# Attention and gated FFN on one core: a new written order, waits between two engines, and tanh queued behind copies

## The chip, the cores and the metric

The kernel runs on one core of a Trainium2 chip. The metric is the device time of one execution in microseconds (us). A core has TensorE (PE: matmuls; PEld: its weight loads), VectorE (DVE), ScalarE (ACT), GpSimd (POOL) and SyncE (SP, which issues most DMAs). Each engine runs its instructions in the order of its own queue; semaphores hold an instruction until another engine's has finished.

## The reference

Block-local attention with block summaries, then a feed-forward layer with a convolution gate, on 4 batches, 8 heads, 768 positions, head size 64 (model width 512, inner width 1024).

```python
def _attn_ref(q, k, v):                      # B, H, S, D = 4, 8, 768, 64
    block, window = (32, 16)
    k_sum = k.reshape(B, H, nb, block, D).max(axis=3)
    v_sum = v.reshape(B, H, nb, block, D).mean(axis=3)
    scores_l = scale * q @ k.T               # kept where |i - j| < window
    scores_s = scale * q @ k_sum.T + np.log(block)
    a = softmax(concat(scores_l, scores_s))
    return a @ concat(v, v_sum)

def _moe_ref(x, w_in, conv_w, w_out):        # x: heads side by side, 512 wide
    h = np.maximum(x @ w_in, 0.0)
    conv_out = sum(conv_w[k] * shifted(h, k - 1) for k in range(3))
    gate = 1.0 / (1.0 + np.exp(-conv_out))
    return (h * gate) @ w_out
```

## The kernel before

The work is cut into 8 chunks (4 batches, two halves of 384 positions each). Attention goes by pairs of heads: pair n belongs to chunk n // 4. The FFN of chunk c runs in 8 units u of 128 inner features. FFN products are split into high and low fp32r parts, so each step of f (first product, `L467`) and of the second product (`L554`) is three matmuls.

The steps have short names, and a written list, ORDER, uses them. Attention: R, K, T, V, Q, M load (SP queue); `ks` takes key maxima over blocks (`L291`, DVE), `vs` value sums (`L307`, DVE), `pv` transposes the sums (`L317`, PE, into the one PSUM bank x), `vm` scales them out of PSUM (`L335`), `kb`, `vb` and `win` copy summaries and key windows into tiles (`L301`, `L341`, `L297`); `qk` is scores (`L354`, PE), `mx` maximum with mask (`L368`, DVE), `ex` exp (`L383`, ACT), `sm`, `rc`, `nr` the normalisation, `tr` the transpose (`L411`, PE), `cp` its copy aT (`L416`), `av` values (`L425`, PE, into bank x), `xh`, `xl` the two parts of x (`L451`, `L455`). Group j of tr and cp is half of pair j // 2. FFN: `f`, `re` relu, `ta` and two `cv` the taps (`L504`), `th` tanh (`L515`, ACT), `mu` the product (`L522`, DVE), `gh` and `gl` its two parts (`L532`, `L535`), `g` a step of the second product, `ob` its way out. Unit (c, u) takes one of three f1 PSUM banks, which is free again after its mu. Weights are unpacked by `z`, `lo` (`L176`), `st` (`L182`), `hi`, `wl` (`L202`). `w` is a number of filler matmuls. A letter at the end of a step (a, v, p) names the engine: ScalarE, VectorE, GpSimd.

Chunks 0 to 2 of the FFN and the attention of pairs 0 to 17 stand in ORDER, and every engine takes that order. From chunk 3 (FIRST) on, a loop emits the units, and there only TensorE's order is as written (`manual_schedule(engines={PE})`); the other queues are ordered by a scheduler that goes by costs. The loop's slot j (j = 8 (c + 1) + 3 + u) loads and prepares: an odd slot vs, pv, vm, ks and kb of pair (j + 1) / 2, an even one the scores and softmax of pair j / 2. In chunk 3 each slot's instructions are put behind the last DMA and the last mu of ORDER on their engine:

```python
with contextlib.ExitStack() as behind:
    if c == FIRST:
        for x in last.values():
            behind.enter_context(tc.issue_after(x))
    slot(j)
```

The first odd slot is 35: pair 18. After it come tr33, the gates (th, mu, gh, gl) of the unit before, the four f steps of unit (3,0) and nine matmuls of the second product; unit (3,1) begins with tr34, av16, slot 36 (qk18) and tr35.

Of the kernel before, what the change touches and what calls it, by code (L numbers as in the profile page):

```python
# [9 lines left out]
F32 = mybir.dt.float32  # L10
# [8 lines left out]
P = 128  # L19
# [73 lines left out]
ex13.0.0 f1.7.3 mx13.1.2 cp23a cv1.6.2 f2.0.1 ex13.0.2 rc12 nr12.0p re1.7 av11 th1.6 gl1.5
ex13.1.1 tr24 mu1.6 ex13.1.2 g2.3 ta1.7v ex13.0.1 nr12.1p f2.0.2 xh11 cv1.7.0 qk14 xl11 cv1.7.2
f2.1.0 K17 cp24v th1.7 g2.4 M15 mx14.0.0 gh1.6 mu1.7 K16 sm13 pv17 gl1.6 f2.0.3 mx14.0.1 T18
mx14.0.2 tr25 re2.0 f2.2.0 ex14.0.1 ta2.0v f2.1.1 gh1.7 mx14.1.0 g2.5 cv2.0.0 ex14.0.0 gl1.7
cp25a mx14.1.1 f2.1.2 cv2.0.2 vm17 g2.6 rc13 th2.0 ks16 nr13.0p ex14.1.0 f2.1.3 ex14.1.1 nr13.1p
mx14.1.2 R18 tr26 mu2.0 f2.2.1 Q16 kb16 gh2.0 pv16 qk15 re2.1 ex14.0.2 g2.7 cp26a mx15.0.0 K18
mx15.0.1 f2.2.2 ta2.1v ob2 f2.3.0 cv2.1.0 f2.2.3 mx15.0.2 cv2.1.2 g3.0 re2.2 vm16 f2.3.1 th2.1
ex14.1.2 tr27 f2.3.2 sm14 mx15.1.0 mx15.1.1 g3.1 mx15.1.2 mu2.1 f2.3.3 ta2.2v gh2.1 g3.2 rc14  # L100
cv2.2.0 nr14.0p av12 cv2.2.2 gl2.0 g3.3 xh12 nr14.1p ex15.0.1 f2.4.0 xl12 ex15.1.1 g3.4 th2.2
cp27a qk16 mu2.2 gh2.2 f2.4.1 re2.3 K19 gl2.2 f2.5.0 ta2.3a f2.4.2 ex15.0.2 kb17 tr28 g3.5
mx16.0.0 mx16.0.1 f2.4.3 cp28v mx16.0.2 g3.6 cv2.3.0 tr29 cv2.3.2 g3.7 mx16.1.0 mx16.1.1 f2.5.1
mx16.1.2 ob3 av13 ex15.0.0 g4.0 ex16.1.0 M17 cp29v ex15.1.2 f2.5.2 V15 ed12 re2.4 Q17 g4.1 xh13
Q18 ex15.1.0 xl13 f2.5.3 M16 ta2.4a g4.2 V16 sm15 th2.3 rc15 V17 cv2.4.0 nr15.1p av14 ex16.0.0
mu2.3 ex16.1.2 nr15.0p cv2.4.2 ex16.1.1 g4.3 ex16.0.1 tr30 gh2.3 g4.4 xh14 gl2.3 re2.5 qk17
# [9 lines left out]
def attention_ffn(ctx, tc, qT, kT, vT, k_win, v_nat, v_win, w_in, cwT, w_out, mask8, ident_in, out):  # L116
# [73 lines left out]
    def lo(kind, fc):  # L190
        lower(f"{kind}{fc}", DM)

    def st(kind, fc):
        joined(f"{kind}{fc}")

    def hi(kind, fc, e="a"):
        copy[e](parts(kind, fc)[0], wu[f"{kind}{fc}"].bitcast(F32))

    def wlo(kind, fc, e="p"):
        h, l = parts(kind, fc)  # L200
        w = wu.pop(f"{kind}{fc}")
        engine[e].tensor_tensor(l, w.bitcast(F32), h.bitcast(F32), ALU.subtract)  # L202
# [7 lines left out]
    def stcw():  # L210
        joined("cw")
# [587 lines left out]
```

## Time and profile before

| | us |
|---|---|
| median of 3 runs | 397.97 |
| the runs | 399.1, 397.97, 394.14 |
| profiled execution, its own time | 394.99 |
| its span, first to last instruction | 393.2 |
| PE, DVE, ACT, POOL busy | 371.7, 255.1, 246.4, 148.4 |
| mean granted TensorE clock | 0.986 |

The span is what the trace covers; the execution's own time has 1.8 us around it. Busy time of an engine is the union of its instructions. Matmuls are pipelined, so a busy TensorE is not one at its peak. The idle time of an engine that sets nothing costs nothing.

### The profile page before, as it was taken

The page shows a single profiled execution, that of the slowest core. Times are in us where ns is not written, and L with a number is a line of the kernel's source. Part 1 is how long each engine was busy: PE and PEld are TensorE (multiplying, and loading weights), DVE is VectorE, ACT ScalarE, POOL GpSimd, SP SyncE. Part 2 cuts the span into 40 slices and gives each one's busy share as a digit, 9 for nine tenths or more (in the row PEclk, how much of TensorE's full clock was granted, in tenths as well). Part 3 has the DMA queues.
Part 4 walks back from the last instruction along what each step waited for, and adds up shares of the span by engine and source line. Part 5 has one row for each costly group of instructions (what it writes and reads, how often), then busy time and mean ns, then how long its engine had stood idle before and what let it go on. Part 6 is the DMA issues. An engine that isn't in the chain of part 4 may idle for free.

```text
span 393.2 us, 8828 instructions
## 1 busy us (share of the span) xinstructions
PE 371.7 (95%) x3167; PEld 316.6 (81%) x3167; DVE 255.1 (65%) x776; ACT 246.4 (63%) x786; POOL 148.4 (38%) x183
## 2 busy tenths in 40 slices
PE   8899889999999992999989999999999999999996
PEld 3677677988888872888978888888988898999884
DVE  5999999997876465667575565466665655566200
ACT  3998989976965576246667777666766743344211
POOL 2756766854442153123323243333333132232200
PEclk9999999999999997699999999999999999999999
DMA  8999947997643660754433323334310000000011
GB/s 302 385 307 320 294 133 249 310 263 248 208 132 110 161 208 28 251 151 161 123 96 114 115 53 98 108 103 124 103 38 28 29 2 27 28 28 27 28 53 53
DMA packets 26859, 55.03 MB, mean 140 GB/s; under 512 B 3072, under 2 KB 11456, under 8 KB 26816
## 3 DMA queue, kind: packets, MB, share of 16 engines
q1 hardware_dynamic: 23072, 47.91, 38.9%
q10 hardware_dynamic: 3744, 6.57, 4.6%
q8 instruction: 25, 0.41, 0.4%
q14 instruction: 18, 0.15, 0.1%
HBM read 46.11 MB, written 6.29 MB: 133 GB/s over the span
## 4 chain that ended last, share of the span: by engine, by line
PE 74%; DVE 11%; DMA 7%; ACT 3%; issue 2%; SPq 1%; POOL 0%; ACTq 0%; DVEq 0%; POOLq 0%
PE f L554 32%; PE f L467 29%; PE xp L425 5%; PE pt L411 5%; PE pq L354 4%; DVE t L504 3%; DMA raw_b<-w_in 2%; DMA raw_a<-w_in 2%; DMA kw<-k_win 1%; DVE a L368 1%; ACT a L383 1%; DVE t L522 1%; DMA mask<-mask 1%; DVE ks L291 1%; ACT t L515 1%
## 5 line engine op out<-in xcount | busy, mean ns | idle before, releaser
L535 POOL TENSOR_TENSOR glo<-t,ghi 128x383 fp32r<-128x383 f32 (+1 forms) x64 | 65.6, 1027 | 122.1 <-ACT ghi L532 114.5
L467 PE MATMUL f<-xh,win_hi 128*128 128x384 f32 (+1 forms) x256 | 92.2, 360 | 0.9 <-DVE t L522 0.5
L467 PE MATMUL f<-xh,win_lo 128*128 128x384 f32 (+1 forms) x256 | 87.1, 340 | 0.0
L467 PE MATMUL f<-xl,win_hi 128*128 128x384 f32 (+1 forms) x256 | 87.1, 340 | 0.0
L504 DVE SCALAR_TENSOR_TENSOR t<-f,cw,t 128x382 f32<-128x382 f32 (+3 forms) x128 | 78.7, 615 | 9.9 <-ACT t L493 7.3
L554 PE MATMUL f<-wout_hi,ghi 128*128 128x512 f32 x192 | 77.2, 402 | 0.0
L383 ACT ACTIVATE a<-a,nm 128x120 f32<-128x120 f32 x192 | 73.5, 386 | 4.2 <-DVE nm L368 3.2
L554 PE MATMUL f<-wout_lo,ghi 128*128 128x512 f32 x192 | 75.6, 394 | 0.0
L554 PE MATMUL f<-wout_hi,glo 128*128 128x512 f32 x192 | 75.3, 393 | 0.0
L403 POOL TENSOR_TENSOR a<-a,sm 128x360 f32<-128x360 f32 x56 | 44.5, 810 | 52.8 <-DVE sm L399 35.4
L515 ACT ACTIVATE t<-t 128x383 f32<-128x383 f32 (+1 forms) x64 | 33.6, 524 | 48.6 <-DVE t L504 47.4
L467 PEld LDWEIGHTS f<-xh,win_hi 128*128 128x128 f32 x256 | 48.8, 191 | 5.9 <-DVE t L522 1.5
L522 DVE SCALAR_TENSOR_TENSOR t<-t,f 128x383 f32<-128x383 f32 (+1 forms) x64 | 35.3, 552 | 26.0 <-ACT t L515 25.7
L368 DVE CUSTOM_DVE_ANT_0 a<-pq,mask 128x120 f32<-128x120 f32 x192 | 44.5, 275 | 10.2 <-PE pt L411 5.3
L467 PEld LDWEIGHTS f<-xl,win_hi 128*128 128x128 f32 x256 | 48.9, 191 | 1.9
L467 PEld LDWEIGHTS f<-xh,win_lo 128*128 128x128 f32 x256 | 48.7, 190 | 0.0
L554 PEld LDWEIGHTS f<-wout_hi,glo 128*128 128x128 f32 x192 | 36.2, 188 | 8.0
L495 DVE TENSOR_SCALAR t<-f,cw 128x385 f32<-128x385 f32 (+1 forms) x42 | 25.9, 617 | 25.1 <-ACT f L482 21.2
L482 ACT ACTIVATE f<-f 128x384 f32<-128x384 f32 (+1 forms) x64 | 30.3, 474 | 17.5 <-PE f L467 17.1
L554 PEld LDWEIGHTS f<-wout_hi,ghi 128*128 128x128 f32 x192 | 36.4, 189 | 5.6 <-ACT ob L564 0.3
L554 PEld LDWEIGHTS f<-wout_lo,ghi 128*128 128x128 f32 x192 | 36.3, 189 | 4.8 <-POOL wout_lo L202 0.2
L532 ACT CAST ghi<-t 128x383 fp32r<-128x383 f32 (+1 forms) x64 | 32.5, 508 | 10.3 <-DVE t L522 10.3
(53 smaller groups left out, 470.6 us busy)
## 6 DMA issues: line engine op xcount, KB each, us to landing
va<-v_win SPq DMA_DIRECT2D x32, 288.0 KB
kw<-k_win SPq DMA_DIRECT2D x24, 360.0 KB
kT<-kT SPq DMA_DIRECT2D x16, 400.0 KB
q<-qT SPq DMA_DIRECT2D x32, 192.0 KB
out_dram<-ob ACTq DMA_DIRECT2D x24, 256.0 KB
vt<-vT SPq DMA_DIRECT2D x12, 384.0 KB
wo<-w_out SPq DMA_DIRECT2D x8, 512.0 KB
raw_a<-w_in SPq DMA_DIRECT2D x6, 512.0 KB
```

The costliest lines, as they stand in the source:

```text
L368: nc.vector.tensor_tensor_reduce(aa[n, h][:, i, :], pq[n][h][:, i * NK : (i + 1) * NK], mask[:, {(0, 0): 0, (1, 2): 2}.get((hf, i), 1), :] ...
L383: nc.scalar.activation(a, a, AF.Exp, bias=nm[n][:, h, i : i + 1], scale=-1.0, accum_out=sm[n][:, h, i : i + 1],)
L403: engine[e].tensor_tensor(a, a, sm[n][:, h, :].unsqueeze(2).to_broadcast([P, 3, NK]), ALU.mult)
L467: nc.tensor.matmul(f1ps[c, u][:, :n], w[:, u, cc, :], x[:, cc, :n], start=(cc == 0 and m == 0), stop=(cc == NCC - 1 and m == 2),)
L482: nc.scalar.activation(h, h, AF.Relu)
L495: nc.vector.tensor_scalar(t, h, cw[:, u, 1:2], 1.0, ALU.mult, ALU.mult)
L504: nc.vector.scalar_tensor_tensor(t[:, i0:i1], f1ps[c, u][:, hf + k - 1 + i0 : hf + k - 1 + i1], cw[:, u, k : k + 1], t[:, i0:i1], ALU.mult ...
L515: nc.scalar.activation(t, t, AF.Tanh, scale=0.5)
L522: return nc.vector.scalar_tensor_tensor(t, t, 1.0, h, ALU.add, ALU.mult)
L532: copy[e](gate_rows("hi", c, u), conv[c, u])
L535: engine[e].tensor_tensor(gate_rows("lo", c, u), conv.pop((c, u)), gate_rows("hi", c, u).bitcast(F32), ALU.subtract,)
L554: nc.tensor.matmul(f2ps[b, st], g[:, fc, ss], w[:, fc, :], start=(fc == 0 and m == 0), stop=(fc == NFC - 1 and m == 2),)
```

## The change

ORDER is written anew: the same steps in another sequence, many with another engine letter, with 30 filler matmuls in place of 35 (12 stand ahead of the list in both). A step may now carry a wait: `a<b` makes step a wait for step b, though it uses nothing of b. There are 43, each between VectorE and GpSimd: 15 hold a VectorE step behind a GpSimd one, 28 the other way. The steps of slot 35 (Q19, vs18, ks18, V18, pv18, vm18, kb18) move into ORDER. In even units of the loop the gates are queued behind the unit's first copy aT on the copy's engine. The functions that make the steps return their instruction so that it can be named; what counts as `last` stays the DMAs and mu.

```diff
 ORDER = """
-R0 Q0 R1 I1 R3 R2 Q1 ks0 I2 win0 T0 kb0 qk0 Q2 win1 ks1 I0 kb1 mx0.0.0 zi1 T1 loi1 mx0.0.1
...
-tr0 vm0 ex1.1.2 qk2 nr0.1v I6 cp0a loi0 sm1 tr1 hii2 mx2.0.0 win6 rc1 mx2.0.1 cp1a pv1 V1
...
-ob4 f2.6.3 sm17 gh2.5 rc17 nr17.0v re2.6 nr17.1p ta2.6a cv2.6.0 gl2.5 f2.7.0 cv2.6.2 gl2.4 th2.6
-f2.7.1 mu2.6 f2.7.2 f2.7.3 re2.7 ta2.7a cv2.7.0 cv2.7.2 th2.7 gh2.6 mu2.7 gl2.6 gh2.7 gl2.7
+R0 Q0 R1 R2 R3 Q1 I2 ks0 I1 Q2 kb0v win0 T0 qk0 ks1 I0 ks2 win2 Q3 win1 mx0.0.0 T1 mx0.0.1
...
+ex0.1.2 ex0.1.1 C loi2<win3 sm0 mx1.0.0 zi2 kb3<loi2 rc0 mx1.0.1 nr0.0p ex1.0.0 mx1.0.2 T2
+mx1.1.0 ex1.0.2 nr0.1p mx1.1.1 w5 tr0 ex1.0.1 mx1.1.2 V1 kb4v qk2 ex1.1.1 sti2<nr0.1p ex1.1.2 Q4
+ex1.1.0 cp0v win5<sti2 mx2.0.0 sm1 w1 tr1 zi1 rc1 loi1<win5 pv0 mx2.0.1 ex2.0.0 nr1.0p<loi1 O0
...
+gl1.7v g2.6 ex14.0.0 Q17 cv2.0.2 ex14.0.2 f2.2.2 ex14.1.2 mx15.0.0 mx15.0.1 av12 cp26a sm14p
...
+gl2.0 mx15.1.1 cv2.2.2 g3.2 xh13 vs17 ex15.1.0 f2.3.2 g3.3 mu2.1 T19 kb16v f2.3.3 mx15.1.2 xl13
+ex15.1.2 tr28 re2.3v qk16 cp28a gh2.1 pv17 f2.4.0 ex15.0.1 mx16.0.0 mx16.0.1 th2.2 g3.4 ex15.1.1
+mu2.2 tr29 sm15p vs18 gh2.2 g3.5 vm17 cp29a M17 f2.5.0 ta2.3v R19 f2.4.1 mx16.0.2 rc15 ex16.0.2
...
+nr16.1p<gl2.3v ex17.1.1 g4.5 xl14 th2.4 gl2.1 ta2.5v tr32 g4.6 mu2.4 cp32a cv2.5.0 ex17.1.0 av15
+sm17 rc17 cv2.5.2 nr17.1p g4.7 th2.5 f2.6.2 xh15 mu2.5 xl15 f2.6.3 re2.6 ta2.6v cv2.6.0 nr17.0v
+f2.7.0 cv2.6.2 gh2.4p<nr17.0v ob4 gl2.4 th2.6 gh2.5v<gl2.4 mu2.6 gl2.5<gh2.5v f2.7.1 f2.7.2
+f2.7.3 re2.7v pv18 ta2.7v cv2.7.0 gh2.6v cv2.7.2 vm18v th2.7 gl2.6v mu2.7 gh2.7 gl2.7
 """
...
-    last = {}
+    last, made = {}, {}
+    held = mybir.DependencyInfo(
+        mybir.DependencyClass.Sync, mybir.DependencyReason.SCHED_ONLY
+    )
...
     def run(text):
+        text, *first = text.split("<")
...
         if x is not None:
-            last[x.ins.engine] = x.ins
+            made[text] = x.ins
+            if name in "KRTQVMOIC" or name == "mu":
+                last[x.ins.engine] = x.ins
+            for y in first:
+                tc.add_manual_dep(x.ins, made[y].name, held, reason="shared port")
...
     def slot_t(j):
         if 0 <= j - 2 < NGROUP:
             tr(j - 2)
-            cpy(j - 2)
+            return cpy(j - 2)
...
     def unit(c, u, pieces):
         j = 8 * (c + 1) + 3 + u
+        copied = None
         if j % 2 == 0:
 
-            slot_t(j)
+            copied = slot_t(j)
             slot_av(j)
         with contextlib.ExitStack() as behind:
             if c == FIRST:
 
                 for x in last.values():
                     behind.enter_context(tc.issue_after(x))
-            slot(j)
+            if c > FIRST or u > 0:
+                slot(j)
         if j % 2 == 0:
             slot_t(j + 1)
         elif c == FIRST and u == 0:
             slot_t(j)
-        gates(1)
+        with contextlib.ExitStack() as behind:
+            if copied is not None:
+
+                behind.enter_context(tc.issue_after(copied.ins))
+            gates(1)
```

## Rows read from the trace of the kernel before

**Rows 1.** The page's busy time in us (share of the span) and instructions of each engine.

```profile
PE 371.7 (95%) x3167; PEld 316.6 (81%) x3167; DVE 255.1 (65%) x776; ACT 246.4 (63%) x786; POOL 148.4 (38%) x183
```

**Rows 2.** Busy time by stretch. Columns: stretch in us from the span's start, its length, then busy us of PE, PEld, DVE, ACT, POOL (instructions begun), granted TensorE clock (1.00 is full), DMA share, GB/s.

```profile
0.00:62.00 62.00, 54.41 (x580) 39.74 (x581) 56.67 (x183) 50.24 (x172) 37.90 (x48) 1.00 0.87 289
62.00:150.00 88.00, 87.75 (x833) 74.30 (x831) 65.81 (x222) 66.06 (x226) 40.22 (x49) 1.00 0.66 202
150.00:158.00 8.00, 0.54 (x3) 0.54 (x4) 5.56 (x9) 4.06 (x10) 4.60 (x5) 0.70 0.08 29
205.00:393.00 188.00, 184.60 (x1374) 162.47 (x1372) 96.17 (x271) 100.09 (x294) 52.34 (x63) 1.00 0.19 61
```

**Rows 3.** The chain that ended last, from 150 to 175 us, in order of time. Columns: start us, us, engine, tile, line, instructions.

```profile
150.05 0.39 ACT f L482
...
152.96 0.39 ACT f L482
...
156.45 0.87 DVE vs L307
...
157.46 0.37 PE pv L317
...
158.47 3.86 PE f L467 x12
162.33 2.65 PE f L554 x9
...
165.31 0.85 PE xp L425 x24
166.16 0.78 PE pq L354 x24
...
167.41 2.12 PE f L467 x12
169.53 2.07 PE f L554 x9
...
175.21 0.33 PE pt L411 x3
```

**Rows 4.** The view of waits over the whole span: who waited for whom, us in total, times, longest us.

```profile
PE pv L317 <- DVE vs L307: 7.7, 1, 7.7
```

**Rows 5.** Two stretches of 2 us behind the hole, columns as in rows 2.

```profile
160.00:162.00 2.00, 2.00 (x8) 2.00 (x7) 0.95 (x1) 0.00 (x0) 0.26 (x1) 0.50 0.94 292
...
164.00:166.00 2.00, 2.00 (x32) 1.61 (x30) 1.57 (x3) 0.48 (x1) 0.00 (x0) 1.00 0.78 251
```

**Rows 6.** The 10 us ahead of the hole, columns as in rows 2.

```profile
140.00:150.00 10.00, 9.75 (x92) 8.07 (x90) 5.11 (x22) 7.40 (x28) 3.54 (x5) 1.00 0.47 139
```

**Rows 7.** The timeline of all engines at the end of ORDER: TensorE's last matmul of f2.7.3. Columns: start us, us, engine, line, operation, tiles, shapes, instructions merged, and in brackets the idle time before and its releaser.

```profile
149.42 0.33 PE L467 MATMUL f<-xh,win_lo 128*128 128x384 f32 x1
```

**Rows 8.** The timeline of PE from 174 to 204 us: the only two rows with an idle time before them.

```profile
177.99 0.51 PE L411 MATMUL pt<-consts,a 128*120 128x128 f32 x3 [0.82 <-ACT aT L416]
201.36 0.52 PE L411 MATMUL pt<-consts,a 128*120 128x128 f32 x3 [1.76 <-ACT aT L416]
```

**Rows 9.** The timeline of ACT ahead of the second of them: tanh (L515) and the copy (L416).

```profile
197.93 0.53 ACT L515 ACTIVATE t<-t 128x385 f32<-128x385 f32 x1 [2.52 <-DVE t L504]
...
200.32 0.53 ACT L515 ACTIVATE t<-t 128x385 f32<-128x385 f32 x1 [0.73 <-DVE t L504]
200.75 0.46 ACT L416 COPY aT<-pt 120x384 f32<-120x384 f32 x1
```

**Rows 10.** The timeline of DVE in the opening: single instructions of nr (L403), st (L182) and lo (L176).

```profile
14.42 0.52 DVE L403 TENSOR_TENSOR a<-a,sm 128x360 f32<-128x360 f32 x1
...
35.39 1.75 DVE L182 SCALAR_TENSOR_TENSOR wu_i<-wu_i,wl_i 128x512 uint32<-128x512 uint32 x1
...
39.36 0.42 DVE L176 TENSOR_SCALAR wl_i<-raw_b 128x512 uint32<-128x512 uint32 x1
...
39.88 0.69 DVE L182 SCALAR_TENSOR_TENSOR wu_i<-wu_i,wl_i 128x512 uint32<-128x512 uint32 x1
...
44.05 1.55 DVE L176 TENSOR_SCALAR wl_o<-wo 128x512 uint32<-128x512 uint32 x1
```

**Rows 11.** The timeline of POOL in the opening.

```profile
35.29 1.31 POOL L202 TENSOR_TENSOR win_lo<-wu_i,win_hi 128x512 fp32r<-128x512 f32 x1
```

**Rows 12.** Groups of instructions by line over the whole span: line, engine, operation, tiles, shapes, count | busy us, mean ns of one | idle us before them, by releaser.

```profile
L182 DVE SCALAR_TENSOR_TENSOR wu_i<-wu_i,wl_i 128x512 uint32<-128x512 uint32 x8 | 7.8, 972 | 0.1
L416 DVE COPY aT<-pt 120x384 f32<-120x384 f32 x14 | 7.7, 550 | 1.9 <-PE xp L425 1.3 <-PE pt L411 0.5
L182 DVE SCALAR_TENSOR_TENSOR wu_o<-wu_o,wl_o 128x512 uint32<-128x512 uint32 x8 | 6.4, 806 | 0.2
L176 DVE TENSOR_SCALAR wl_o<-wo 128x512 uint32<-128x512 uint32 x8 | 5.3, 662 | 0.0
L403 DVE TENSOR_TENSOR a<-a,sm 128x360 f32<-128x360 f32 x8 | 5.2, 650 | 0.0
L335 ACT ACTIVATE vm<-pv 24x128 f32<-24x128 f32 x16 | 4.0, 259 | 2.9 <-PE pv L317 2.3 <-ACT ob L564 0.4
L176 DVE TENSOR_SCALAR wl_i<-raw_a 128x512 uint32<-128x512 uint32 x6 | 3.7, 614 | 0.0
L297 DVE COPY kw<-kT 128x576 f32<-128x576 f32 x1 | 0.5, 450 | 0.0
```

More of the change, by code (lines that the diff above doesn't have):

```diff
@@ L95 @@
[L95 to L106, printed above, removed]
@@ new lines @@
+mx13.1.2 nr12.0v gh1.5 f2.0.2 M15 ex13.1.0 mu1.6 qk14 ex13.1.1 ta1.7v ex13.0.0 g2.2 cv1.7.0 K17
+tr24 nr12.1v M14 f2.1.0 cv1.7.2 M13 gl1.5<nr12.1v cp24a g2.3 xh11 mx14.0.0 mx14.0.1 th1.7 xl11
+f2.1.1 ex13.1.2 ed12 g2.4 ex14.0.1 gh1.6v sm13 mx14.0.2 gl1.6<gh1.6v kb15v tr25 pv16 f2.1.2
+mx14.1.0 mu1.7 g2.5 vm16v mx14.1.1 f2.1.3 mx14.1.2 rc13 ks17 nr13.1p f2.0.3 re2.1 f2.2.0 cp25a
+nr13.0p ta2.1v re2.0 qk15 cv2.1.0 gh1.7p ta2.0a tr26 ex14.1.1 cv2.0.0 Q19 f2.2.1 ex14.1.0 K18
+gl1.7v g2.6 ex14.0.0 Q17 cv2.0.2 ex14.0.2 f2.2.2 ex14.1.2 mx15.0.0 mx15.0.1 av12 cp26a sm14p
@@ new lines @@
+cv2.1.2 th2.0 mx15.0.2 g2.7 mu2.0 M16 xh12v gh2.0p tr27 ob2 f2.2.3 cp27v f2.3.0 mx15.1.0 th2.1
+ks18 g3.0 ex15.0.0 re2.2 rc14 f2.3.1 xl12 nr14.0p ex15.0.2 g3.1 ta2.2a nr14.1p av13 cv2.2.0
+gl2.0 mx15.1.1 cv2.2.2 g3.2 xh13 vs17 ex15.1.0 f2.3.2 g3.3 mu2.1 T19 kb16v f2.3.3 mx15.1.2 xl13
+ex15.1.2 tr28 re2.3v qk16 cp28a gh2.1 pv17 f2.4.0 ex15.0.1 mx16.0.0 mx16.0.1 th2.2 g3.4 ex15.1.1
+mu2.2 tr29 sm15p vs18 gh2.2 g3.5 vm17 cp29a M17 f2.5.0 ta2.3v R19 f2.4.1 mx16.0.2 rc15 ex16.0.2
+cv2.3.0 g3.6 mx16.1.0 cv2.3.2 f2.4.2 nr15.0v f2.5.1 mx16.1.1 kb17<nr15.0v g3.7 mx16.1.2 kb18
@@ new lines @@
+nr15.1v<kb18 tr30 ob3 qk17 gl2.2<nr15.1v f2.5.2 th2.3 mx17.0.0 ex16.0.0 av14 mx17.0.1 mx17.0.2
+cp30a ex16.1.0 g4.0 ex16.0.1 V18 ex16.1.1 f2.4.3 V16 ex17.0.0 V15 g4.1 re2.4v ex16.1.2 Q18 xh14
+tr31 mu2.3 V17 g4.2 ta2.4v cp31a K19 ex17.0.1 mx17.1.0 f2.6.0 sm16v gh2.3 rc16 g4.3 nr16.0v
+ex17.0.2 cv2.4.0 f2.5.3 mx17.1.1 g4.4 mx17.1.2 re2.5 gl2.3v ex17.1.2 f2.6.1 cv2.4.2
+nr16.1p<gl2.3v ex17.1.1 g4.5 xl14 th2.4 gl2.1 ta2.5v tr32 g4.6 mu2.4 cp32a cv2.5.0 ex17.1.0 av15
+sm17 rc17 cv2.5.2 nr17.1p g4.7 th2.5 f2.6.2 xh15 mu2.5 xl15 f2.6.3 re2.6 ta2.6v cv2.6.0 nr17.0v
@@ L190, in lo @@
     def lo(kind, fc):
-        lower(f"{kind}{fc}", DM)
+        return lower(f"{kind}{fc}", DM)
     def st(kind, fc):
-        joined(f"{kind}{fc}")
+        return joined(f"{kind}{fc}")
     def hi(kind, fc, e="a"):
-        copy[e](parts(kind, fc)[0], wu[f"{kind}{fc}"].bitcast(F32))
+        return copy[e](parts(kind, fc)[0], wu[f"{kind}{fc}"].bitcast(F32))
     def wlo(kind, fc, e="p"):
@@ L210, in stcw @@
     def stcw():
-        joined("cw")
+        return joined("cw")
     def C():
@@ L296, in win @@
         k = bass.AP(tensor=k.tensor, offset=k.offset, ap=[list(k.ap[0]), [QB, CB], [1, WK]])
-        engine[e if n else "v"].tensor_copy(keys(n)[:, :, :WK], k)
+        return engine[e if n else "v"].tensor_copy(keys(n)[:, :, :WK], k)
     def kb(n, e="p"):
         c, p, b, hf = at(n)
-        engine[e].tensor_copy(
+        return engine[e].tensor_copy(
             keys(n)[:, :, WK:NK], ks[b, p].unsqueeze(1).to_broadcast([P, CB, NB])
@@ L340, in vb @@
         c, p, b, hf = at(n)
-        engine[e].tensor_copy(
+        return engine[e].tensor_copy(
             va[n][WK:NK, :, :], vm[b, p].unsqueeze(1).to_broadcast([NB, CB, P])
@@ L402, in nr @@
         a = aa[n, h]
-        engine[e].tensor_tensor(
+        return engine[e].tensor_tensor(
             a, a, sm[n][:, h, :].unsqueeze(2).to_broadcast([P, 3, NK]), ALU.mult
@@ L531, in gh @@
     def gh(c, u, e="a"):
-        copy[e](gate_rows("hi", c, u), conv[c, u])
+        return copy[e](gate_rows("hi", c, u), conv[c, u])
     def gl(c, u, e="p"):
-        engine[e].tensor_tensor(
+        return engine[e].tensor_tensor(
             gate_rows("lo", c, u),
```

104 lines of the change are left out of this document (50 added, 54 removed).

## The prediction

> **What bounds the kernel now.** I read the busy shares first [rows 1], then the same by stage [rows 2], then the chain that ended last around the stage that stands out [rows 3]. TensorE is busy 95% of the span, and from 205 us to the end it waits for next to nothing (184.6 of 188 us, the rest is the tail), so there only less TensorE work would help, and the change removes none. Time can come from earlier places. In the first 62 us VectorE sets the pace: 56.7 busy of 62, while TensorE works in bursts. From 62 to 150 us TensorE is busy 87.75 of 88 us, VectorE 65.8. From 150 to 158 us TensorE does 0.54 us of work: a hole, and the granted clock goes down in it. Behind it TensorE has two waits worth naming, 2.6 us together [rows 8].
>
> **The hole.** The chain shows what fills it [rows 3]: ScalarE starts re2.6 at 150.05; taps, tanh and products of units 2.6 and 2.7 run one after another until mu2.7 ends at 156.45; only then comes vs18 (L307, 0.87 us), and TensorE's next instruction, pv18 (L317), at 157.46: a wait of 7.7 us on vs18 [rows 4]. It is no lack of work: behind pv18 stand tr33 and the 12 matmuls of f(3,0), whose inputs were made before. In the code the issue_after of chunk 3 puts vs18 behind the last mu on VectorE, and TensorE takes its own order as written, so one small transpose holds everything.
>
> The clock row stands beside it [rows 5]: 1.00 before [rows 2], 0.50 by 160 to 162 us, 1.00 again after 164. Those are its two levels, 1.2 and 2.4 GHz. What that took is read from equal work at either level [rows 3]: 12 matmuls of f in 3.86 us against 2.12 later, 9 of the second product in 2.65 against 2.07: 1.74 + 0.58 = 2.3 us.
>
> **Part 1, the first slot in the written order.** Q19, vs18, ks18, V18, pv18, vm18 and kb18 leave the loop. On VectorE vs18 and ks18 now stand among chunk 2's last units, some 0.9 us each, where VectorE is busy about half of the time, 5.1 of the last 10 us [rows 6]; without that cover they would cost 1.8 us. Of the DMAs, Q19 and V18 go into SP's queue ahead of the loop's; I cost them at nothing, since what the loop loads next is due units later (if V18 waited for its buffer for long, those loads would be late behind it). pv18 stays right behind f2.7.3 on TensorE, but its input is old by then. So 7.7 + 2.3 = 10.0 us go.
>
> What is late next? f(3,0) needs a free f1 bank, so mu2.5; f(3,1) needs mu2.6, f(3,2) mu2.7; av16 needs the x bank that vm18 empties. From the end of f2.7.3 TensorE has pv18 and tr33 (0.37 + 0.33), f(3,0) and its second product (2.12 + 2.07) and tr34 (0.33), which is 5.2 us to av16; then 0.85 + 0.78 + 0.33, 7.2 us to f(3,1); then f(3,1) itself, 9.3 us and more to f(3,2) [rows 3]. In the hole mu2.7 came 3.5 us behind re2.7 (152.96 to 156.45); the new list puts re2.7, ta2.7, gh2.6, gl2.6 and vm18 on VectorE, three of them between, at some 0.5 us each: about 5 us against 9.3. vm18 stands behind five instructions of some 0.55 on VectorE and takes 0.26 [rows 12]: 3.0 us against 5.2. f(3,0) is the tightest: mu2.5 now stands just ahead of f2.6.3, four f steps and pv18 and tr33 ahead of f(3,0), about 2.8 us by f steps of 0.53 (a quarter of 2.12). In the trace re2.6 started after even the last matmul of f2.7.3 (149.42 and 0.33) [rows 7], four steps behind its own, because of exps and ob4 in ScalarE's queue. The new list has the exps earlier, but a like delay of 2 to 3 us would show here. Bounds 0 to 3 us; I take 0.5, near zero since each margin is positive: **minus 9.5 us**.
>
> **Part 2, tanh behind copies.** In even units the loop's gates (tanh and gh on ScalarE) are queued behind that unit's copy aT. TensorE's two waits after the hole are for just that copy, 0.82 and 1.76 us [rows 8]. At the second ScalarE sat in a tanh that waited for VectorE's taps until 197.93, did another at 200.32, and the copy only at 200.75 [rows 9]. The tanh that waits first may belong to the unit before, which the new edge doesn't touch; then only the last 0.43 us leaves the path. Bounds 0 to 2.6 us, I take the middle: **minus 1.3 us**. What now stands behind the copy is tanh, so mu and the f1 bank of a later unit; the copy follows a transpose that opens the unit, so tanh moves by about one copy. From 205 us on TensorE's own work hides this; without that cover it would be half a microsecond per even unit.
>
> **Part 3, the opening: another order, other engines, 43 waits.** The waits join VectorE and GpSimd only (24 of them before f0.6.0: ten hold VectorE behind GpSimd, 14 the other way). Behind a held VectorE instruction stand the maxima, the taps and mu, so exp on ScalarE and TensorE's f banks wait too; behind a held GpSimd instruction stand nr (the transposes) and gl. What they are about is visible [rows 10]: wu_i took 1.75 us at 35.39 against 0.69 at 39.88, and wl_o 1.55 at 44.05 against 0.42 for wl_i; at 35.29 a GpSimd instruction of 1.31 us began [rows 11]. Over the groups [rows 12] the excess over the undisturbed length is 8 x (0.972 - 0.69) + 8 x (0.806 - 0.69) + 8 x (0.662 - 0.42) + 6 x (0.614 - 0.42) + 8 x (0.650 - 0.52) = 2.3 + 0.9 + 1.9 + 1.2 + 1.0 = 7.3 us, nearly all on the engine that sets the pace. A wait turns a stretch into idle time of the same engine; it gains only where it lets the short instruction go first. Ten waits at 0 to 1.3 us are 0 to 13 us against 7.3: from minus 7.3 to plus 5.7.
>
> The Trainium skill, in "SBUF — State Buffer", section "Who interferes with whom", says that the port pair that VectorE and GpSimd share is a lock held for a whole instruction, so whoever starts first blocks the other. By that rule a wait in itself wins nothing, and this term would be zero. The rows agree as far as they go: what stretches grows by about one GpSimd instruction.
>
> VectorE's own load ahead of f1.0.0, counted in both lists: it gains 6 kb, 4 vb, 3 vm, 2 wl, 4 sm, one vs, one hi, and loses 4 cp, 7 nr, 2 st and one each of lo, ta, cv. The one SBUF copy of such a kind on VectorE took 0.45 us for 576 columns [rows 12]; kb has 144, so 0.1 to 0.45, I take 0.2; vb has 768, so 0.6; wl as nr by columns, 0.74; vm and sm at most 0.26; vs 0.87; hi 0.4: 1.2 + 2.4 + 1.8 + 1.5 + 0.9 + 0.4 = 8.2. What leaves, with ta and cv at the 0.55 of cp: 4 x 0.55 + 7 x 0.52 + 2 x 0.69 + 0.42 + 2 x 0.55 = 8.7. Net minus 0.5 us, with 2 either way. TensorE's work ahead of f1.0.0 is less by one qk (0.78) and one second-product step (2.07 / 3 = 0.69) and more by one tr (0.33), 1.1 us that it must do later, when it is the bound. So the plan by itself is even; the filler matmuls, 30 for 35, free nothing, as they fill waits. For the whole part I take **minus 1 us**, a little under zero as the waits are placed one by one; bounds plus 6 to minus 7.
>
> **Sum.** 394.99 (span 393.2 and 1.8 around it) - 9.5 - 1.3 - 1.0 = 383.2, so **383 us**. The profiled execution lies 3 us under the median of the runs, 397.97, which run from 394.1 to 399.1; no row shows what made two of them longer, so the upper side gets more room. A change of less than about 2% (8 us) can hardly be told from none here.
>
> **The rivals.** (a) The hole moves: the engines used it to catch up, and TensorE stops at f(3,0) or av16 instead. Half of the 7.7 us back and half of the clock's 2.3: 383 + 3.9 + 1.2 = 388. For it: re2.6 was late by over 2 us at 150. Against: VectorE idles a quarter of the time from 62 to 150 us [rows 2]. (b) The waits cost more than they save: ten at 1.3 us less 7.3, and the 1 us I had taken: 383 + 6.7 = 390. For it: VectorE paces the whole opening, and the kb and vb copies new on it read and write SBUF as GpSimd's do. The skill's lock rule points the same way. (c) Slower: the clock falls in the opening. The new list has f steps earlier against VectorE's work and fewer filler matmuls; if a gap there gets long enough, what follows runs at half clock. Price: 12 matmuls took 1.74 us more on 2.12, so 30 us of TensorE work behind f0.0.0 would take 25 us more: 383 + 25 = 408. It decides somewhere between the gap that left the clock full (1.76 us at 201.36) [rows 8] and the 7.7 us that did not. (d) vs18 or pv18 is held by something else, a late load say, and the hole stays: 393.
>
> **How the numbers follow.** The forecast 0.70 (own range 376 to 389), (a) 0.12, (b) 0.12, (c) 0.04, (d) 0.02. Range 375 to 391: it takes in (a) and (b) and leaves out (c), (d) and the far ends. Two per cent under the median is 390: the forecast lies under it, most of (a) and half of (b): faster 0.81, same 0.14, slower 0.05.
>
> **What will show it.** Right: no wait of TensorE on vs; TensorE busy nearly all of what was 150 to 158 us; the clock at 1.00 throughout; no wait of TensorE on aT over 1 us. Part 3: the means of wu, wl and a on VectorE nearer to 0.69, 0.42 and 0.52, and VectorE's idle time in the opening grown by less than 7.3 us. Wrong: a new TensorE wait of some us on mu (L522), vm or xl at the same place, or an opening that ends later than 62 us.

## The result and the profile after

The changed kernel takes 383.16 us (median; 382.53 to 384.18) against 398.17 of the kernel before in the same comparison: a ratio of 0.964, 95% interval 0.957 to 0.971. The forecast was 383 us. By these medians the gain is 15.0 us, where the forecast took 11.8 off a profiled execution of 394.99; the kernel before ran from 394.14 to 399.10 here, and its medians in the later comparisons are 395.45 to 396.32. The profiled execution of the changed kernel took 383.44 us, with a span of 381.7 us, 11.5 less than before. The page's busy time of the changed kernel, and its stretches as in rows 2 (the same columns):

```profile
PE 369.4 (97%) x3162; PEld 315.0 (83%) x3162; DVE 259.3 (68%) x810; ACT 235.1 (62%) x758; POOL 137.6 (36%) x177
```

```profile
0.00:62.00 62.00, 55.09 (x586) 40.38 (x586) 54.97 (x199) 50.49 (x168) 34.49 (x47) 1.00 0.86 281
62.00:150.00 88.00, 87.95 (x836) 75.19 (x836) 75.22 (x240) 61.46 (x209) 35.84 (x49) 1.00 0.73 224
150.00:158.00 8.00, 6.29 (x69) 5.25 (x68) 7.22 (x21) 3.11 (x8) 2.72 (x3) 0.86 0.18 47
158.00:205.00 47.00, 47.00 (x403) 41.88 (x402) 32.48 (x103) 30.45 (x108) 16.34 (x22) 0.99 0.50 152
205.00:381.70 176.70, 173.09 (x1275) 152.27 (x1273) 89.39 (x250) 89.58 (x269) 48.25 (x58) 1.00 0.18 59
```

From 150 to 158 us TensorE now works 6.29 us where it worked 0.54 [rows 2], but not 8, and the clock is at 0.86. TensorE's timeline shows why:

```profile
147.78 0.33 PE L472 MATMUL f<-xh,win_lo 128*128 128x384 f32 x1
147.95 0.27 PE L322 MATMUL pv<-consts,vs 128*24 128x128 f32 x1
148.06 0.49 PE L416 MATMUL pt<-consts,a 128*120 128x128 f32 x3
148.31 0.42 PE L472 MATMUL f<-xh,win_hi 128*128 128x386 f32 x1
...
154.77 0.92 PE L430 MATMUL xp<-aT,va 120*64 120x64 f32 x24 [1.71 <-DVE vm L342]
```

pv18 follows f2.7.3 at once: the wait of 7.7 us [rows 4] is gone. f(3,0) runs at 148.31 without a wait. The next step, av16 (xp, L430), waits 1.71 us for vm18, and then qk18 takes 1.32 us (in the chain below) where it took 0.78 [rows 3]: the clock has halved. The windows show the two levels, 2.4 and 1.2 GHz:

```profile
154.00:156.00 2.00, 1.23 (x35) 1.17 (x39) 2.00 (x6) 0.79 (x2) 0.00 (x0) 0.94 0.00 0
156.00:158.00 2.00, 2.00 (x26) 1.70 (x21) 2.00 (x10) 1.20 (x4) 1.00 (x1) 0.50 0.72 188
```

The 11.5 us can be laid out along TensorE's sequence, since the two kernels do the same work there from f2.7.3 on.

- **To the end of f2.7.3:** 149.42 [rows 7] is now 147.78, minus 1.64. I put that down to part 3; one trace of each kernel is thin ground, but six traces with the new order, its waits and part 1 have 147.78 to 148.36, and two with the old order and the slot in the loop 149.42 and 150.29.
- **To the first second product behind the slow clock:** in the chain it began at 169.53 [rows 3] and now begins at 160.62, minus 8.91. So part 1 brought 8.91 - 1.64 = 7.3 us.
- **To the transpose that waited longest for aT:** 201.36 [rows 8] is now 189.81, minus 11.55. So part 2, with what the shift brings, gave 2.6 us. No wait on aT is left there.

The chain's row and the timeline's:

```profile
160.62 2.08 PE f L559 x9
```

```profile
189.81 0.55 PE L416 MATMUL pt<-consts,a 128*120 128x128 f32 x3
```

**Why vm18 is late.** The chain that ended last, in order of time, around the wait:

```profile
138.95 6.12 DMA kw<-k_win
...
145.19 0.31 POOL kw L306
...
145.53 0.95 DVE ks L296
...
149.10 0.52 POOL ghi L537
...
149.69 1.03 POOL glo L540
...
151.56 0.49 DVE f L489
...
154.53 0.20 DVE vm L342
...
154.77 0.92 PE xp L430 x24
155.69 1.32 PE pq L359 x24
```

re2.7 (f, L489) could have started when f2.7.3 was done, at 148.1, and started at 151.48 on VectorE. Two things stand before it. A ks of chunk 4, an instruction of the loop, stands ahead of mu2.5 in VectorE's queue and was held by a kw that waited for its load; VectorE was idle 1.14 us, then worked 0.95 on it. And gh2.5 waits for gl2.4, one of the 43 new waits: idle 1.19 us more. VectorE's timeline has both (in brackets: idle before, and the releaser):

```profile
145.53 0.95 DVE L296 TENSOR_REDUCE ks<-kT 128x24 f32<-128x768 f32 x1 [1.14 <-POOL kw L306]
...
150.74 0.36 DVE L537 CAST ghi<-t 128x383 fp32r<-128x383 f32 x1 [1.19 <-POOL glo L540]
...
151.48 0.56 DVE L489 TENSOR_SCALAR f<-f 128x384 f32<-128x384 f32 x1
...
154.44 0.27 DVE L342 TENSOR_SCALAR vm<-pv 24x128 f32<-24x128 f32 x1
```

**The opening.** VectorE's groups that rows 12 show stretched are all but undisturbed now (busy us, mean ns, idle before):

```profile
L187 DVE SCALAR_TENSOR_TENSOR wu_o<-wu_o,wl_o 128x512 uint32<-128x512 uint32 x8 | 5.5, 690 | 0.6 <-POOL a L408 0.2
L187 DVE SCALAR_TENSOR_TENSOR wu_i<-wu_i,wl_i 128x512 uint32<-128x512 uint32 x8 | 5.5, 688 | 0.3
L181 DVE TENSOR_SCALAR wl_o<-wo 128x512 uint32<-128x512 uint32 x8 | 3.5, 440 | 0.0
L408 DVE TENSOR_TENSOR a<-a,sm 128x360 f32<-128x360 f32 x6 | 3.2, 528 | 0.3 <-POOL kw L306 0.2
L181 DVE TENSOR_SCALAR wl_i<-raw_a 128x512 uint32<-128x512 uint32 x6 | 2.6, 427 | 0.4 <-POOL win_hi L202 0.2
```

wu_i fell from 972 to 688 ns, wl_o from 662 to 440, wl_i from 614 to 427, a from 650 to 528. Summed over all VectorE instructions of the first 62 us against the short ones of their form (what lies over 0.1 us), the stretch fell from some 8.7 to 3.8 us, while idle time, 62 us less the busy time, rose from 5.3 to 7.0 us. Of the 3.8, some 3 lie on the kb and vb copies, which are new on VectorE: they took 523 and 867 ns in the mean, where the prediction had 0.2 and 0.6 us.

### The profile page after: what moved, and what is told of

Read it like the earlier page. It is cut to its first block, busy times and chain, and to the rows that moved or that the text cites. A ratio compares the mean times of both kernels' runs of the same rounds, so it can differ in the third digit from the quotient of the medians.

```text
span 381.7 us, 8826 instructions
## 1 busy us (share of the span) xinstructions
PE 369.4 (97%) x3162; PEld 315.0 (83%) x3162; DVE 259.3 (68%) x810; ACT 235.1 (62%) x758; POOL 137.6 (36%) x177
## 3 DMA queue, kind: packets, MB, share of 16 engines
HBM read 46.11 MB, written 6.29 MB: 137 GB/s over the span
## 4 chain that ended last, share of the span: by engine, by line
PE 79%; DVE 11%; issue 2%; DMA 2%; POOL 2%; SPq 1%; ACT 1%; DVEq 0%; POOLq 0%
PE f L559 33%; PE f L472 30%; PE xp L430 6%; PE pq L359 5%; PE pt L416 5%; DVE t L509 2%; DMA kw<-k_win 2%; DVE wu_i L187 1%; DVE a L373 1%; DVE t L527 1%; DVE wu_o L187 1%; DVE ks L296 1%; POOL a L408 1%; SPq L284 1%; DVE kw L306 1%
## 5 line engine op out<-in xcount | busy, mean ns | idle before, releaser
L540 POOL TENSOR_TENSOR glo<-t,ghi 128x385 fp32r<-128x385 f32 (+1 forms) x60 | 60.4, 1015 | 121.9 <-ACT ghi L537 105.6
L388 ACT ACTIVATE a<-a,nm 128x120 f32<-128x120 f32 x192 | 73.7, 387 | 12.6 <-DVE nm L373 11.8
L520 ACT ACTIVATE t<-t 128x383 f32<-128x383 f32 (+1 forms) x64 | 32.5, 524 | 30.2 <-DVE t L509 28.6
L487 ACT ACTIVATE f<-f 128x386 f32<-128x386 f32 (+1 forms) x60 | 28.5, 475 | 35.4 <-PE f L472 35.3
L527 DVE SCALAR_TENSOR_TENSOR t<-t,f 128x383 f32<-128x383 f32 (+1 forms) x64 | 34.4, 551 | 15.7 <-ACT t L520 15.6
L421 ACT COPY aT<-pt 120x384 f32<-120x384 f32 x59 | 27.9, 473 | 20.5 <-PE pt L416 20.4
```

The source lines that it names most:

```text
L388: nc.scalar.activation(a, a, AF.Exp, bias=nm[n][:, h, i : i + 1], scale=-1.0, accum_out=sm[n][:, h, i : i + 1],)
L421: return copy(aT[j][:NK, :], pt.pop(j)[:NK, : 3 * P])
L487: nc.scalar.activation(h, h, AF.Relu)
L520: nc.scalar.activation(t, t, AF.Tanh, scale=0.5)
L527: return nc.vector.scalar_tensor_tensor(t, t, 1.0, h, ALU.add, ALU.mult)
L540: return engine[e].tensor_tensor(gate_rows("lo", c, u), conv.pop((c, u)), gate_rows("hi", c, u).bitcast(F32), ALU.subtract,)
```

## The experiments

The median of the kernel before lay between 395.45 and 396.32 us in the three comparisons below, so the ratios are the safer measure across them. The changed kernel itself stands at 0.964 above and at 0.972 in the second of these comparisons. In the first (the next four runs) and the third it did not run, so these ratios alone do not tell a difference of 0.01 or less from none.

**Part 1 undone.** Slot 35 goes back into the loop, and its seven steps leave ORDER, with the one wait that names one of them (`nr15.1v<kb18`):

```diff
-            if c > FIRST or u > 0:
-                slot(j)
+            slot(j)
```

> The changed kernel with part 1 alone undone: the seven steps of slot 35 are out of the written order and back in the loop, behind the last mu. My theory: the hole comes back, TensorE waits some 7 us for vs18 and the clock falls in it (2.3 us more), while the changed kernel's own wait of 1.7 us at av16 and the 1.5 us of slow clock behind it go: 383.2 + 7.5 + 2.3 - 3.2 = 390. Rival: the hole came from engines that were late, which the new order mended, and the place of vs18 matters little: 384 to 386, a wait on vs18 of under 3 us.

390.81 us, ratio 0.986 (0.981 to 0.990). The hole is back, in the view of waits:

```profile
PE pv L319 <- DVE vs L309: 7.5, 1, 7.5
```

So the place of vs18 makes the hole, whatever the rest of the order.

**Part 2 undone.** The gates no longer queue behind the copy:

```diff
-            if copied is not None:
+            if False:
```

> The changed kernel with part 2 alone undone: the loop's gates are no longer queued behind the copy aT. Theory: TensorE's waits on aT come back between 158 and 205 us, 1.3 to 2.6 us: 384.5 to 386. Rival: the 2.5 us that the changed kernel won between its f(3,0) and 205 us came from the earlier loads and sums of slot 35, and the copies are on time without the edge: 383.

386.61 us, ratio 0.976 (0.971 to 0.981), a little more than expected. TensorE waits for aT again, and ScalarE's timeline shows what the copy (L421) stands behind:

```profile
191.99 0.51 PE L416 MATMUL pt<-consts,a 128*120 128x128 f32 x3 [1.88 <-ACT aT L421]
```

```profile
188.56 0.53 ACT L520 ACTIVATE t<-t 128x385 f32<-128x385 f32 x1 [2.63 <-DVE t L509]
...
190.95 0.53 ACT L520 ACTIVATE t<-t 128x385 f32<-128x385 f32 x1 [0.73 <-DVE t L509]
191.38 0.46 ACT L421 COPY aT<-pt 120x384 f32<-120x384 f32 x1
```

In the changed kernel the same stretch of ScalarE reads:

```profile
188.64 0.53 ACT L520 ACTIVATE t<-t 128x385 f32<-128x385 f32 x1 [2.94 <-DVE t L509]
189.07 0.46 ACT L421 COPY aT<-pt 120x384 f32<-120x384 f32 x1
189.43 0.53 ACT L520 ACTIVATE t<-t 128x385 f32<-128x385 f32 x1
```

The edge puts the second tanh behind the copy, and with it the product and taps that this tanh waits for: the copy comes 2.3 us earlier, though the slow clock had set TensorE's sequence back by 1.6 us in that execution and not in this one.

**The 24 waits ahead of f0.6.0 taken out**, the order and the engines kept (two of the 24):

```diff
-ex0.1.2 ex0.1.1 C loi2<win3 sm0 mx1.0.0 zi2 kb3<loi2 rc0 mx1.0.1 nr0.0p ex1.0.0 mx1.0.2 T2
+ex0.1.2 ex0.1.1 C loi2 sm0 mx1.0.0 zi2 kb3 rc0 mx1.0.1 nr0.0p ex1.0.0 mx1.0.2 T2
```

> The changed kernel without the 24 added waits ahead of f0.6.0; the order and the engines stay. Theory by the lock (whoever comes second waits a whole instruction with or without a semaphore): the stretches of wu, wl and a on VectorE come back, its idle time falls by as much, and the time stays at 383, within 1 us. Rival 1: the waits put the short instruction first, and without them the opening ends 2 to 4 us later: 385 to 387. Rival 2: they cost more than they save: 381 or less.

387.18 us, ratio 0.977 (0.973 to 0.981). wu_i is stretched as before, and TensorE pays for it: an aT late by 2 us, and the clock down behind it:

```profile
L183 DVE SCALAR_TENSOR_TENSOR wu_i<-wu_i,wl_i 128x512 uint32<-128x512 uint32 x8 | 7.7, 959 | 0.3
```

```profile
46.85 0.90 PE L412 MATMUL pt<-consts,a 128*120 128x128 f32 x3 [1.98 <-ACT aT L417]
```

```profile
48.00:52.00 4.00, 4.00 (x19) 4.00 (x18) 4.00 (x12) 3.98 (x14) 1.98 (x2) 0.72 0.02 6
```

The last of f2.7.3 comes 4.7 us later than in the changed kernel. The reading that a wait only turns a stretch into idle time has fallen: without these waits the stretch is some 9.4 us against 3.8, and VectorE's idle time of the first 62 us 6.6 against 7.0. That the waits do it by letting the short instruction go first fits (14 of the 24 put a GpSimd instruction behind one of VectorE), but was not followed instruction by instruction.

**The other 19 waits taken out**, in the same way (`gh2.5v<gl2.4` becomes `gh2.5v`, and so on).

> The changed kernel without the 19 added waits behind f0.6.0. Theory: VectorE's idle 1.2 us ahead of gh2.5 (it waits for gl2.4, which waits for gh2.4, which waits for nr17.0) goes, vm18 comes 1 us earlier, and TensorE's wait at av16 falls from 1.7 to some 0.5 us, with less slow clock behind it: 381 to 382. Rival: the port holds gh2.5 just as long as the semaphore does: 383.

385.61 us, ratio 0.973 (0.969 to 0.977). The wait on vm falls from 1.7 to 0.8 us, but f2.7.3 comes 3.6 us later: from 62 to 90 us TensorE works 25.54 us, against 27.95 in the changed kernel. So the time is no better: the 1 to 2 us that I expected to win are not there, and a loss is not told from none.

```profile
62.00:90.00 28.00, 25.54 (x229) 21.15 (x228) 27.45 (x75) 22.50 (x70) 15.79 (x18) 1.00 0.78 250
```

**The changed kernel again**, beside the next three.

> The changed kernel as it is, beside the three that follow: 383, within 1 us, so that they are compared on the same chip.

384.70 us (383.04 to 385.14), ratio 0.972 (0.967 to 0.976). Its wait on vm is 1.77 us, a little longer than the 1.71 above, and yet the clock stays up:

```profile
155.16 0.92 PE L430 MATMUL xp<-aT,va 120*64 120x64 f32 x24 [1.77 <-DVE vm L342]
```

```profile
156.00:158.00 2.00, 2.00 (x36) 1.83 (x33) 2.00 (x7) 1.07 (x3) 0.90 (x1) 1.00 0.59 137
```

**The loop's ks held back:** chunk 4's first VectorE instructions go behind the last mu of chunk 2.

```diff
             if c == FIRST:
 
                 for x in last.values():
                     behind.enter_context(tc.issue_after(x))
+            if c == FIRST + 1:
+                behind.enter_context(tc.issue_after(last[mybir.EngineType.DVE]))
```

> The changed kernel with one more edge: chunk 4's slots on VectorE are queued behind the last mu too, as chunk 3's are. In the changed kernel's trace a key maximum of the loop (ks24) stands in VectorE's queue between cv2.5.2 and mu2.5, where it waits 1.1 us for GpSimd's kb20, which waits for a load. Theory: that wait and the 0.9 us of the reduction are why vm18 is late; without them VectorE is 1.5 to 2 us earlier, TensorE's 1.7 us wait at av16 goes and the slow clock behind it: 2 to 3 us less than the changed kernel, 380 to 381. Rival: the wait gh2.5 behind gl2.4 takes over and vm18 comes as late: 383.

383.21 us, ratio 0.967 (0.962 to 0.971). The ks is gone from its place, but VectorE now waits 0.65 us for re2.6, so that nr17.0 and, behind it, gh2.4 and gl2.4 on GpSimd come hardly earlier. VectorE still stands before gh2.5 until gl2.4 is done, and vm18 starts at 154.34 instead of 154.44. As f2.7.3 came 0.58 us later in this execution, TensorE's wait at av16 is 1.03 us and not 1.71:

```profile
150.64 0.36 DVE L537 CAST ghi<-t 128x383 fp32r<-128x383 f32 x1 [1.18 <-POOL glo L540]
...
154.34 0.27 DVE L342 TENSOR_SCALAR vm<-pv 24x128 f32<-24x128 f32 x1
```

```profile
154.67 0.92 PE L430 MATMUL xp<-aT,va 120*64 120x64 f32 x24 [1.03 <-DVE vm L342]
```

So the ks made up some 0.7 us of the wait, and the chain through gl2.4 holds the rest. The median is 1.5 us below that of the changed kernel in the same comparison, but the two intervals overlap.

**vm18 on ScalarE:**

```diff
-f2.7.3 re2.7v pv18 ta2.7v cv2.7.0 gh2.6v cv2.7.2 vm18v th2.7 gl2.6v mu2.7 gh2.7 gl2.7
+f2.7.3 re2.7v pv18 ta2.7v cv2.7.0 gh2.6v cv2.7.2 vm18 th2.7 gl2.6v mu2.7 gh2.7 gl2.7
```

> The changed kernel with vm18 on ScalarE in place of VectorE. ScalarE is idle about half of the time there, so vm18 ends some 2 us earlier whatever VectorE waits for. Theory: the wait at av16 is about vm18 alone; it goes, with the slow clock behind it: 2 to 3 us less than the changed kernel, 380 to 381. Rival: the next thing late, mu2.6 or mu2.7 on the same VectorE, holds f(3,1) for as long: 383.

381.07 us, ratio 0.962 (0.958 to 0.965): the best time of the study, 3.6 under the changed kernel of the same comparison. vm18 runs in ScalarE's gap, and the two steps that stood behind it run without a wait and at full clock:

```profile
150.35 0.25 ACT L337 ACTIVATE vm<-pv 24x128 f32<-24x128 f32 x1
```

```profile
153.32 0.92 PE L427 MATMUL xp<-aT,va 120*64 120x64 f32 x24
154.16 0.84 PE L356 MATMUL pq<-kw,q 64*64 64x120 f32 x24
```

**All 43 waits taken out**, the two edits of ORDER above together.

> The changed kernel without any of the 43 added waits. The early 24 alone were worth 4 us and the late 19 some 2.4. Theory: each saves where it stands, the new order leans on all of them, and the two add up: 388 to 390, with TensorE's last step of chunk 2 some 8 us later than with them. Rival: they make up for one another, and without both it is no worse than without the early ones: 387.

389.20 us, ratio 0.982 (0.978 to 0.986): 4.5 us over the changed kernel of the same comparison. The last of f2.7.3 comes 7.6 us later than in the changed kernel and 6.0 later than in the kernel before. wu_i is at 956 ns. The new order without its waits opens no better than the old one did, by this trace worse.

**Each part alone on the kernel before.** Part 1 (the loop leaves slot 35 out, and the seven steps are set into the old list, for example):

```diff
-cv2.2.0 nr14.0p av12 cv2.2.2 gl2.0 g3.3 xh12 nr14.1p ex15.0.1 f2.4.0 xl12 ex15.1.1 g3.4 th2.2
-cp27a qk16 mu2.2 gh2.2 f2.4.1 re2.3 K19 gl2.2 f2.5.0 ta2.3a f2.4.2 ex15.0.2 kb17 tr28 g3.5
+av12 cv2.2.2 gl2.0 g3.3 xh12 nr14.1p ex15.0.1 f2.4.0 xl12 ex15.1.1 g3.4 th2.2 cp27a qk16 mu2.2 vs18
+gh2.2 f2.4.1 re2.3 K19 gl2.2 f2.5.0 ta2.3a f2.4.2 ex15.0.2 kb17 kb18 tr28 g3.5 mx16.0.0 mx16.0.1
```

> Part 1 alone on the kernel before: the eight steps of slot 35 stand in the old written order (Q19 behind Q18, ks18 behind th2.1, vs18 behind mu2.2, V18 behind tr30, kb18 behind kb17, pv18 behind re2.7, vm18 behind cv2.7.2), the loop leaves the slot out; old order, no added waits, tanh not held. The prediction's sum for this part is 9.5 us: 386.5 against a kernel before of 396, with TensorE waiting nowhere over 0.5 us between f(2,7) and the loop. The theory that the changed kernel's own trace suggests, that a residual moves to av16 behind vm18, gives 6 to 8 us: 388 to 390, with a wait of 1.5 to 3 us on vm. The rival that the part needs the room which the new order makes (VectorE is fuller at 140 to 150 us in the old one) gives under 5 us: 391 or more, with a wait on vs, ks or vm over 3 us.

387.83 us, ratio 0.980 (0.975 to 0.986), so 7.8 us (5.7 to 9.8). The old order leaves the same residual at the same place, in TensorE's timeline:

```profile
160.18 0.92 PE L423 MATMUL xp<-aT,va 120*64 120x64 f32 x24 [1.53 <-DVE vm L335]
```

This profiled execution's f2.7.3 lies 3.95 us behind that of the kernel before, 1.7 of it already at f0.6.0, ahead of any step of slot 35; it is the longest of its four (386.31 to 390.22), so the median is read and not its span. From f2.7.3 on it can be laid beside the kernel before: to the second product behind qk18 it takes 10.95 us in TensorE's timeline against 19.95, 9.0 less, at full clock.

Part 2 (the gates held, and nothing else; `slot_t` returns the copy):

```diff
-        gates(1)
+        with contextlib.ExitStack() as behind:
+            if copied is not None:
+                behind.enter_context(tc.issue_after(copied.ins))
+            gates(1)
```

> Part 2 alone on the kernel before: the gates queue behind the unit's first copy aT on the copy's engine, all else as before. The prediction's term is 1.3 us (0 to 2.6): 394.7 against 396. The theory from the two traces and from the run without this part (2.5 to 3.6 us, the slow clock behind the gap included) gives 392.4 to 393.5, with no wait on ACT aT over 1 us. A rival: in the old kernel, whose units lie otherwise, holding the gates delays a mu and loses what it wins: 396.

393.75 us, ratio 0.9946 (0.9921 to 0.9971), so 2.1 us (1.2 to 3.1). No wait of TensorE is left between 174 and 204 us; the copy that came at 200.75 [rows 9] comes at 198.29, directly behind the first tanh:

```profile
197.86 0.53 ACT L515 ACTIVATE t<-t 128x385 f32<-128x385 f32 x1 [3.14 <-DVE t L504]
198.29 0.46 ACT L416 COPY aT<-pt 120x384 f32<-120x384 f32 x1
```

Part 3 (the changed kernel with both of the first two edits above, so with 42 waits):

> Part 3 alone: the new written order with its 43 waits, slot 35 back in the loop, tanh not held. The prediction's term is 1 us (395 against 396); the last matmul of f2.7.3, 1.6 us earlier in the changed kernel, gives 394.4 if nothing of that comes from the other parts. A rival: the order's gain ends in the hole that part 1 closes (pv18 waits for vs18, which stands in the loop behind the opening's last steps on VectorE); then what the opening wins makes the wait longer, and the time is 396 or above, with a wait of pv on vs of 7.7 us or more.

394.55 us, ratio 0.9948 (0.9924 to 0.9972), so 2.1 us (1.1 to 3.0). The hole is there as ever (7.5 us on vs). The rival that the hole eats what the opening wins is not borne out by the time. In the profiled execution f2.7.3 comes 0.6 us later than in that of the kernel before. But it lost 1.5 us to the clock in the opening: behind an idle stretch of 1.96 us, which the changed kernel has too and passes at full clock, it took 6.44 us from the av in the first row to f0.1.2, against 4.89 there.

```profile
33.20 0.92 PE L427 MATMUL xp<-aT,va 120*64 120x64 f32 x24 [1.96 <-issue]
```

```profile
36.00:38.00 2.00, 2.00 (x8) 1.79 (x6) 1.79 (x4) 1.06 (x2) 0.01 (x1) 0.50 0.89 199
```

Nor could these two traces show all of the gain: the kernel before was profiled at 394.99 us, 1.3 under its median of this comparison, and this run at 394.58.

**vm18 on ScalarE and the ks held**, the two diffs together:

> The changed kernel with vm18 on ScalarE and chunk 4's first VectorE instructions held behind the last mu of chunk 2, both at once. With vm18 off VectorE alone the time was 381.07 and the next wait of TensorE was 0.8 us for a mu; with chunk 4's ks held VectorE comes free 1 to 2 us earlier for these mu. Theory that VectorE is still last there: 379.5 to 380.5, no wait on mu over 0.3 us. Rival that GpSimd's gl (gl2.4 and gl2.5) is last after vm18 is moved: 381, the same as with vm18 moved alone.

382.01 us, ratio 0.965 (0.962 to 0.968): no better than with vm18 moved alone. VectorE's steps come 0.7 us earlier, but TensorE was already full there with vm18 moved:

```profile
150.00:154.00 4.00, 4.00 (x40) 3.41 (x40) 2.96 (x7) 1.55 (x4) 1.99 (x2) 1.00 0.10 22
```

(That row is of the kernel with vm18 moved alone.) So neither VectorE nor GpSimd was last there any more, which neither side of the expectation had said. The wait of 0.8 us for a mu that the expectation builds on stands at 58.55 us, in the opening.

## Why the prediction was right, and where its steps were not

The three parts alone give 7.8 + 2.1 + 2.1 = 12.0 us; predicted were 9.5 + 1.3 + 1.0 = 11.8, and the two traces differ by 11.5. The parts add up within their intervals, some 2.5 us either way together (an estimate from the three intervals), so a part that lives on another by less than that isn't ruled out. The total came out so close because misses of opposite sign cancel, which is luck. Two of the prediction's own signs failed: the clock is not at 1.00 throughout, and there is a new wait on vm at the old place, of 1.71 us.

- **The hole (part 1): the mechanism was right, the residual was mis-sized.** The 7.7 us and the slow clock behind it went as said. The residual, taken as 0.5 us at f(3,0), was 1.71 us of waiting at av16 and, in the profiled execution, 1.6 us of halved clock: in the chain qk18 began 166.16 - 155.69 = 10.47 us earlier than before [rows 3], the second product behind it only 8.91. The step that failed is the start of re2.7. I had 5.2 us of TensorE work from f2.7.3 to av16; it was 148.11 to 153.05, 4.9. I had 3.0 us from re2.7 to the end of vm18; it was 151.48 to 154.71, 3.2. But I let re2.7 start at once, and it started 3.4 us late. I had named such a delay of 2 to 3 us for f(3,0), with its small margin, and not carried it to av16, whose margin of 2.2 us it also exceeds. Rival (a) had this place, at 3.9 us and 1.2 of clock; 1.7 and 1.6 came. In four other profiled executions with a wait on vm of 1.5 to 1.8 us the clock part is missing.
- **The clock's price behind the hole** was taken as 2.3 us from 21 matmuls. From f2.7.3 to the second product behind qk18 the kernel before took 19.95 us in TensorE's timeline; with vm18 on ScalarE, without a wait, it takes 9.33. So the hole cost 10.6 us, 7.7 of waiting and 2.9 of clock. In three other executions with the same hole the clock's part was 1.6 to 2.2.
- **Part 2: mis-sized, 1.3 us taken, 2.1 measured alone.** Along TensorE's sequence it is 2.6 us, in the changed kernel and in the run of part 2 alone: the upper end of the bounds. I left open whether the tanh that waits first would be moved; the first was not, and the second, with its wait for taps, was. It was this second one that held the copy, so nearly the whole wait went and not half.
- **Part 3: near in size (1.0 taken, 2.1 measured alone, 1.64 in the two traces), wrong in its reasons.** I took the plan for even and the waits for nearly nothing. On top of parts 1 and 2 the 43 waits are worth 4.5 us, and without them the kernel wins 7.1 us (0.982 of 396), where parts 1 and 2 alone sum to 9.9. So the plan by itself looks no better than even; by these medians it is 2.8 us worse, about as much as the intervals leave open, and the new order without its waits was not run on the kernel before. The sum of excesses [rows 12], 7.3 us, was the right measure of what could go, since nearly all of those groups' stretch went; and the price, idle time, was 1.7 us where I had let it reach 13.
- **The rule of the Trainium skill** ("SBUF — State Buffer", "Who interferes with whom"): that the issue order decides who blocks agrees with this, since waits that change who goes first took wu_i from 959 to 688 ns. My inference from the lock, that a wait in itself wins nothing, does not: with the order fixed, the engine that sets the pace loses less.
- **Rival (b)**, waits that cost more than they save, is refuted: of the three runs without waits none is faster, and the one without all 43 is 4.5 us slower. **Rival (c)**, a clock that falls in the opening, is not in the profiled execution of the changed kernel (1.00 to 150 us), but it is real. With part 1 undone and with part 3 alone the same opening lost 1.5 us to it, behind the idle stretch of 1.96 us. In the run without the early waits the clock was at 0.72 from 48 to 52 us, 0.28 of 4 us, so about 1 us there. The price was thus 1 to 2 us and not 25, since the clock did not stay down: it was at 1.00 again from 52 us in that run, from 40 us with part 3 alone. Nor does the length of the gap decide between 1.76 and 7.7 us, as I had it: 1.71 us halved the clock once, and 1.96 us twice. **Rival (d)** is out: the wait on vs is gone.

What stays open: why the clock falls behind one gap and not behind another of the same length; and how far the late waits pay by themselves, since the run without them (384.82 to 386.35) overlaps the changed kernel's second set (383.04 to 385.14).

## What to carry to other kernels

When a wait of many us goes, follow each later consumer back to the start of its chain, and give every chain the same delay that the trace already shows for one of them; a margin is safe only if it exceeds that. Two engines whose instructions stretch one another are planned by order: sum a group's excess over its undisturbed length to see what ordering can win, and fix by a wait who goes first. A single small instruction in the queue of a full engine can hold the one that bounds the kernel; moving it to an engine with a gap (vm18, 0.25 us on ScalarE) gave more than shortening the full queue (3.6 us against 1.5, which the intervals don't tell from nothing). Before a part's gain is read from two traces, lay several executions of the same kernel beside each other: here the opening alone moved by over a microsecond.

## What the runs showed of the hardware that I had not expected

- Gaps of the same length left TensorE's clock at either level. After 1.71 us of waiting it was at 0.50; in another execution of the same kernel, after 1.77 us, at 1.00; 1.76 us in the kernel before [rows 8] also left it at 1.00. The 1.96 us in the opening left it at 1.00 in both executions of the changed kernel and took it to 0.50 with part 1 undone and with part 3 alone. So a stall of this size has two prices here, about 1.5 us apart, and one profile shows one of them.
- The same hole of 7.5 to 7.7 us cost between 1.6 and 2.9 us of slow clock in four executions.
- Stretch and idle time are not exchanged one for one: with the same order, the 24 early waits took some 5.6 us of stretch off VectorE in the first 62 us for 0.4 us more of idle time.
